# One head of an output projection, loaded by a transfer of 123 rows and one of 5 instead of with its fifteen neighbours

## The chip, the core and the metric

The kernel runs on one core of one Trainium2 chip. The metric is the device time of one execution in microseconds (us). A core has five engines that run side by side, each with its own list of instructions: TensorE (PE, matmuls; its weight loads are shown as PEld), VectorE (DVE), ScalarE (ACT), GpSimd (POOL) and SyncE (SP), which here mostly issues transfers. The transfers themselves run on 16 DMA engines that all queues share. Data is brought from the chip's large memory (HBM) into SBUF, which has 128 partitions; matmul results go to PSUM.

## What is computed

Two independent attention blocks, A and B, with one query token each, decode a cache of 8192 positions; their results stand side by side in the output.

```python
def _A_ref(x, k_cache, v_cache, wq, wo):          # _B_ref: the same with its own arrays
    B, Sq, D = x.shape                             # 1, 1, 512
    H, Dh = 32, 128
    q = (x @ wq).reshape(B, Sq, H, Dh).transpose(0, 2, 1, 3)
    scores = einsum("bhqd,bhkd->bhqk", q, k_cache) * (Dh ** -0.5)   # k_cache: 1, 32, 8192, 128
    p = softmax(scores, axis=-1)
    o = einsum("bhqk,bhkd->bhqd", p, v_cache)
    return o.transpose(0, 2, 1, 3).reshape(B, Sq, H * Dh) @ wo      # wo: 4096 x 512
out = concatenate([a, b], axis=-1)                 # 1, 1, 1024, bf16
```

All inputs are bf16. Each block reads 64 MB of K, 64 MB of V, 4 MB of wq and 4 MB of wo.

## The kernel before

The 32 heads of each block are worked on in tiles of four heads, so there are NM = 16 tiles, n = 0 to 7 for A and 8 to 15 for B. A tile of K or V is 128 partitions by T = 256 positions by 128 numbers: each head fills 32 partitions, and each partition holds 64 KB in one piece of HBM. K has two buffers (`kn`), V one (`vn`).

For each tile, DVE multiplies K by the query in four chunks (`plan_mul`, L343), PE folds the products with an identity matrix (`plan_red`, L352), DVE finishes the sums (`plan_sr`, L363) and takes the maximum, ACT does the exponentials (`plan_exp`, L400). PE then multiplies the probabilities with the V tile in 256 matmuls (`plan_pv`, L421), and DVE scales the result (`plan_o`, L430). PE and DVE run this as loops over the tiles; SP and ACT have it written out.

All loads are issued by SP in a fixed order, in one queue, and each waits on SP until the buffer it overwrites is free. On the DMA engines a queue keeps its order: each engine works through its part of one transfer and then goes on to its part of the next. A transfer over 128 partitions is carried by all 16 DMA engines, eight partitions each.

The end of the order is what the change touches. The two wo arrays are loaded into the K buffer that has come free by then. Block A's wo is one transfer of 32 heads, 32 KB per partition. Block B's wo is cut into groups of heads, `WOG[1]`: heads 0 to 15, then 16 to 23, 24 to 27, 28 and 29, 30, and 31. Within a group of n heads the 128 n rows of wo are dealt to the partitions in runs of n rows, so that each partition holds n KB in one piece; `o` is brought into the same order on PE (`plan_relayout`, L469 to L478) before it is used. SP's order there is: A's wo, B's group 0 (`BEFORE = 1` group), then, when PE is done with the V tile before, the last V tile in two parts (`VLAST`: 192 and 64 positions), then B's groups 1 to 5. Group 0 is used by `plan_wo(1, 0)` (L489), 64 matmuls, ahead of the last V tile; groups 1 to 5 by `plan_wo_rows` (L519), 64 matmuls, behind it. Then DVE copies the result (L530), and it is stored by two transfers of two rows each, one issued by SP and one by ACT (`plan_out`); A's half has been stored earlier in the same way by two transfers from ACT.

`load_wo(a, g)` (L289 to L293) issues the load of one group. It counts up the group's own semaphore, `s_wo[a][g]`, by 16 when the data is there; `wo_in[a, g]` keeps the count to wait for. `dma` (L246, L247) is the helper that issues every transfer, so all of them have L247 in the profile.

Of the kernel before, what the change touches and what calls it, by code (L numbers as in the profile page):

```python
# [11 lines left out]
P = 128  # L12
# [11 lines left out]
class _Plan:  # L24
# [6 lines left out]
    def wait(self, eng, mark):  # L31
        if mark is None:
            return
        ctr, val = mark
        if val <= 0 or self.waited.get((eng, ctr.name), 0) >= val:
            return
        self.waited[(eng, ctr.name)] = val
        self.prog[eng].append((None, ctr, val))

    def op(self, eng, fn, ctr=None, needs=(), inc=1):  # L40

        for m in needs:
            self.wait(eng, m)
        self.prog[eng].append((fn, ctr, inc))
        if ctr is None:
            return None
        ctr.n += inc
        return ctr, ctr.n
# [81 lines left out]
def bass_concat_heads__mha_block_cached__gqa_block_cached__decode_kernel(  # L130
# [21 lines left out]
    NOUT = wos[0].shape[1]  # L152
# [9 lines left out]
    NM = NA * QA  # L162
    NK = 2
    CT = 64
    NCH = T // CT
# [2 lines left out]

    WOG = [[(0, 32)], [(0, 16), (16, 8), (24, 4), (28, 2), (30, 1), (31, 1)]]
    BEFORE = 1  # L170
    HT = [32, 16]
    RG = [32, 16, 8, 4, 2]
    VLAST = (0, T - CT, T)

    with ExitStack() as st:
        ec = st.enter_context

        def sb(name, shape, dt):
            return ec(nc.sbuf_tensor(name, shape, dt))
# [4 lines left out]
        def flat(ap):  # L184
            return ap.rearrange("p t d -> p (t d)")
# [6 lines left out]
        wo_sb = [flat(kn[:, KW])[:, a * W:(a + 1) * W].rearrange("p (j n) -> p j n", n=NOUT)  # L192
                 for a in range(NA)]
# [17 lines left out]
        o2 = sb("o2", [P, NA, H], BF16)  # L211
        oz = sb("oz", [P, H - HT[1], P // 4], BF16)
        mask = {g: sb("mask%d" % g, [P, P // g], BF16) for g in RG}
# [20 lines left out]
        def ctr(name):  # L234
            return _Ctr(nc, st, name)
# [3 lines left out]
        s_wo = [[ctr("s_wo%d%d" % (a, i)) for i in range(len(WOG[a]))] for a in range(NA)]  # L239
# [6 lines left out]
        def dma(eng, dst, src, c, needs=()):  # L246
            return op(eng, lambda e: e.dma_start(dst, src), c, needs, inc=16)  # L247
# [21 lines left out]
        k_in, v_in, wq_in, wo_in = {}, {}, {}, {}  # L269
        red_done, pv_done, q_done, wo_done = {}, {}, {}, {}  # L270
# [18 lines left out]
        def load_wo(a, g):  # L289
            h0, n = WOG[a][g]  # L290
            src = wos[a][h0 * Dh:(h0 + n) * Dh, :].rearrange("(p j) n -> p (j n)", p=P)
            wo_in[a, g] = dma("SP", wo_sb[a][:, h0:h0 + n, :].rearrange("p j n -> p (j n)"), src,
                              s_wo[a][g], [red_done[NM - 2, NCH - 1]])  # L293


        load_wq(0)
# [2 lines left out]
        for a in range(NA):  # L299
# [6 lines left out]
            m = op("PE", xmm, c_pe, [x_in, i_onesb])  # L306
# [122 lines left out]
        def plan_o(n):  # L429
            o_done[n] = op("DVE", lambda e: e.tensor_tensor(  # L430
                oD[:].rearrange("p a h -> p (a h)")[:, nth(n, G)], acc[:, 0:G],
                rinv[:, nth(n), :].rearrange("p o g -> p (o g)"), ALU.mult),
                c_dve, [pv_done[n], r_done[n]])
# [12 lines left out]
        def o_for(a, h0, n):  # L446
            if h0 < HT[a]:
                return o2[:, a, h0:h0 + n]
            return oz[:, h0 - HT[a]:h0 - HT[a] + n, QR - 1]

        def plan_o_rows(a, h0):

            o2_ready[a] = op("DVE", lambda e: e.tensor_copy(o_for(a, h0, H - h0), oD[:, a, h0:H]),
                             c_dve, [i_oz, o_done[NM - 1]])
# [5 lines left out]
        def plan_relayout(*groups):  # L460
            assert len(groups) <= 2
            made = []
            for a, g in groups:
                h0, n = WOG[a][g]
                z = z_n[0] % 2
                z_n[0] += 1
                s = P // n
                zv = zb[:, z, :].rearrange("p (h s) -> p h s", s=s)
                made.append((a, g, h0, n, z, op("DVE", lambda e, a=a, h0=h0, n=n, s=s, zv=zv: e.tensor_tensor(  # L469
                    zv, oD[:, a, h0:h0 + n].unsqueeze(2).broadcast_to([P, n, s]),  # L470
                    mask[n][:, None, :].broadcast_to([P, n, s]), ALU.mult),
                    c_dve, [sel_ready[n], o_done[a * QA + (h0 + n - 1) // G], z_free.get(z)])))
            for a, g, h0, n, z, m in made:
                z_free[z] = op("PE", lambda e, n=n, z=z: e.matmul(  # L474
                    z_ps[z][:, 0:n], zb[:, z, :], jsel[n][:], start=True, stop=True),
                    c_pe, [m, z_read[z][0]])
            for a, g, h0, n, z, m in made:
                o2_ready[a, g] = z_read[z][0] = op("DVE", lambda e, a=a, h0=h0, n=n, z=z: e.tensor_copy(  # L478
                    o_for(a, h0, n), z_ps[z][:, 0:n]), c_dve, [z_free[z], i_oz])

        def plan_wo(a, g):
# [3 lines left out]
            def mm(e):  # L485
                r = None
                for j in range(h0, h0 + n):
                    for i in range(NQ):
                        r = e.matmul(qyp[:, i:i + 1], wo_sb[a][:, j, i * P:(i + 1) * P],  # L489
                                     o2[:, a, j:j + 1], start=(j == 0 and i == 0),  # L490
                                     stop=(j == HT[a] - 1 and i == NQ - 1), skip_group_check=True)
                return r
# [4 lines left out]
        def yrow_of(a):  # L497
            return yrow[:, a * P:(a + 1) * P]

        def plan_turn(a):  # L500

            qy_free[0] = op("DVE", lambda e: e.tensor_copy(
                yT[:].rearrange("p (u r) -> p u r", u=NQ // 2)[:, :, QR - 1:QR + 1],
                qyp[:, 0:NQ].rearrange("p (u r) -> p u r", u=NQ // 2)), c_dve,
                            [i_yT, wo_done[a], yr_done.get(a - 1)])
            yr_done[a] = op("PE", lambda e: e.matmul(
                yrow_of(a), yT[:], ident_f[:], start=True, stop=(HT[a] == H),
                skip_group_check=True), c_pe, [qy_free[0], i_identf])

        def plan_wo_rows(a, g):  # L510

            h0, n = WOG[a][g]

            def mm(e):
                r = None
                for j in range(h0, h0 + n):
                    for i in range(NQ):
                        m = QR - QR * (i % 2) + i % 2
                        r = e.matmul(yrow[i * QR:i * QR + m, a * P:(a + 1) * P],  # L519
                                     oz[:, j - HT[a], QR - m:QR],  # L520
                                     wo_sb[a][:, j, i * P:(i + 1) * P], start=False,
                                     stop=(j == H - 1), skip_group_check=True)
                return r
            yr_done[a] = op("PE", mm, c_pe, [o2_ready[a, g] if n > 1 else o2_ready[a],
                                            wo_in[a, g]])
# [23 lines left out]
        for n in range(NM):  # L549
# [3 lines left out]
            if n + 1 < NM:  # L553
                load_k(n + 1)
            else:
                load_wo(0, 0)
                for g in range(BEFORE):
                    load_wo(1, g)
# [28 lines left out]
        early = [g for g, (h0, n) in enumerate(WOG[1]) if h0 + n <= H - G]  # L587
        for g in range(BEFORE, NB):
            load_wo(1, g)
# [8 lines left out]
        plan_turn(1)  # L598
        plan_relayout(*[(1, g) for g in early[BEFORE:]])
        wait("PE", misc_free[0])  # L600
# [6 lines left out]
        plan_o(NM - 1)  # L607
        plan_wo_rows(1, BEFORE)
        plan_relayout(*[(1, g) for g in range(len(early), NB) if WOG[1][g][1] > 1])
        plan_o_rows(1, WOG[1][NB - 2][0])  # L610
        for g in range(BEFORE + 1, NB):
            plan_wo_rows(1, g)
# [85 lines left out]
```

## Time and profile before

| | |
|---|---|
| median of 3 runs | 666.4 us (666.21 to 666.71) |
| the profiled execution | 666.43 us, its span 665.2 us |
| moved by DMA | 285.33 MB in 6076 packets, mean 429 GB/s |
| busy: PE, PEld, DVE, ACT, POOL | 442.8, 254.9, 340.4, 62.4, 3.0 us |
| mean granted TensorE clock | 0.762 of full speed |

The span reaches from the first instruction of the core to its last; the rest of the execution's time lies around it. Line numbers such as L421 are those of the kernel's file. A row of the timeline gives the start, the duration, the engine, the line, the instruction and the tiles (written<-read), the count, and in brackets the idle time of the engine before it with what ended it. The view of the DMA engines gives, for a window of time that is asked for, the packets that started in it: their number and bytes, how many were under 512 B, 2 KB and 8 KB, and for each queue the time that its packets took as a share of all 16 engines' time. q1 is SP's queue and q10 ACT's; q8 and q14 carry instructions. A row of the table of windows gives the window, its length, then the busy time and number of instructions of PE, PEld, DVE, ACT and POOL, the granted clock, and last the share of time in which the DMA engines were busy (1.00 is all sixteen) and GB/s.

### The profile page before, as it was taken

What the parts mean: (1) busy time and instruction counts of PE and PEld (TensorE: products, weight loads), DVE (VectorE), ACT (ScalarE), POOL (GpSimd) and SP (SyncE); (2) the same over time, 40 slices, a digit from 0 to 9 for tenths busy, and PEclk for the clock granted to TensorE, in tenths of its full rate; (3) what the DMA queues carried; (4) which work ended last, traced back from release to release, by engine and by line L of the source; (5) the groups of instructions that cost most, each with busy time, mean ns of one, the idle gap of its engine ahead of it and who ended that gap; (6) DMA issues with size and microseconds to landing.
All of it is one profiled execution on the core that took longest, in us unless ns stands there. A gap on an engine that the chain in (4) does not pass through costs nothing. (4 is left out here: it accounts for less than half of the span.)

```text
span 665.2 us, 12459 instructions
## 1 busy us (share of the span) xinstructions
PE 442.8 (67%) x5649; PEld 254.9 (38%) x5649; DVE 340.4 (51%) x217; ACT 62.4 (9%) x151; POOL 3.0 (0%) x14
## 2 busy tenths in 40 slices
PE   1165876948487594848759484865948386594885
PEld 0022342615235261614426161442626144262655
DVE  1095809366391836639183663908366380825610
ACT  1002002020201002020100202010020202002020
POOL 1000000000000000000000000000000000000000
PEclk9998857769787766978776597877659787765875
DMA  9999999999999999999999999999999999999997
GB/s 378 441 441 438 438 432 422 418 441 434 434 437 441 441 426 414 441 434 434 437 441 437 426 418 441 434 434 437 441 437 426 418 441 434 434 437 441 404 437 315
DMA packets 6076, 285.33 MB, mean 429 GB/s; under 512 B 690, under 2 KB 948, under 8 KB 1204
## 3 DMA queue, kind: packets, MB, share of 16 engines
q1 hardware_dynamic: 6056, 285.22, 99.3%
q8 instruction: 6, 0.10, 0.1%
q14 instruction: 2, 0.02, 0.0%
q10 hardware_dynamic: 12, 0.00, 0.0%
HBM read 285.21 MB, written 0.00 MB: 429 GB/s over the span
## 5 line engine op out<-in xcount | busy, mean ns | idle before, releaser
L352 PE MATMUL rps<-kn,ident 128*128 128x512 bf16 x1024 | 292.9, 454 | 165.9 <-DVE kn L343 165.9
L343 DVE TENSOR_TENSOR kn<-kn,qbc 128x8192 bf16<-128x8192 bf16 x64 | 281.5, 4419 | 96.1 <-DMA kn<-in_A_k_cache_dram 55.9
L352 PEld LDWEIGHTS rps<-kn,ident 128*128 128x128 bf16 x1024 | 112.2, 113 | 333.6 <-issue 258.3
L421 PE MATMUL acc<-pt,vn 128*128 128x4 bf16 x4096 | 109.4, 165 | 9.8 <-issue 4.1
L421 PEld LDWEIGHTS acc<-pt,vn 128*128 128x128 bf16 x4096 | 108.6, 101 | 10.7 <-DMA vn<-in_B_v_cache_dram 4.5
L363 DVE TENSOR_REDUCE s_sb<-rps 128x64 f32<-128x512 f32 x64 | 44.0, 688 | 110.2 <-PE rps L352 110.2
L400 ACT ACTIVATE pt<-s_sb,negb 32x256 bf16<-32x256 f32 x64 | 54.9, 857 | 1.9
L392 ACT ACTIVATE negb<-bmp 128x1 f32<-128x1 f32 x16 | 2.7, 171 | 529.1 <-PE bmp L388 529.1
L430 DVE TENSOR_TENSOR oD<-acc,rinv 128x4 f32 (+1 forms) x16 | 2.6, 162 | 96.2 <-PE acc L421 85.5
L388 PE MATMUL bmp<-gm,hrow 1*128 1x1 f32 x128 | 18.5, 261 | 6.0 <-DVE gm L378 6.0
L388 PEld LDWEIGHTS bmp<-gm,hrow 1*128 1x128 f32 x128 | 17.2, 204 | 10.7 <-DVE gm L378 10.0
L375 PE MATMUL mtp<-ident_f,m 128*1 128x128 f32 x32 | 6.1, 271 | 19.8 <-DVE m L369 19.8
L400 ACT ACTIVATION_READ_ACCUMULATOR pt<-s_sb,negb 32x1 f32 x64 | 15.9, 248 | 0.0
L375 PEld LDWEIGHTS mtp<-ident_f,m 128*1 128x1 f32 x32 | 1.4, 81 | 27.7 <-DVE m L369 27.7
L303 PE MATMUL misc<-ones_bf,kn 1*128 1x128 bf16 x4 | 0.6, 305 | 13.2 <-DMA kn<-in_B_x_dram 13.2
L378 DVE TENSOR_REDUCE gm<-mtp 1x4 f32<-1x128 f32 x16 | 4.4, 278 | 7.5 <-PE mtp L375 7.5
L405 PEld LDWEIGHTS misc<-rsum,ones_f 128*128 128x128 f32 x32 | 6.2, 197 | 3.6 <-issue 1.4
L321 PE MATMUL qyp<-vn,xb 128*32 128x512 bf16 x64 | 6.0, 504 | 2.2 <-ACT qbc L329 1.5
L369 DVE TENSOR_REDUCE m<-s_sb 128x1 f32<-128x256 f32 x16 | 6.7, 420 | 0.5
L489 PE MATMUL qyp<-o,kn 128*128 128x1 bf16 x192 | 5.5, 165 | 1.0 <-issue 0.8
L489 PEld LDWEIGHTS qyp<-o,kn 128*128 128x128 bf16 x192 | 5.4, 102 | 1.3 <-issue 0.8
L329 ACT CAST qbc<-qyp 128x512 bf16<-128x512 f32 x4 | 2.3, 585 | 37.6 <-PE qyp L321 37.6
(41 smaller groups left out, 31.2 us busy)
## 6 DMA issues: line engine op xcount, KB each, us to landing
vn<-in_B_v_cache_dram SPq DMA_DIRECT2D x1, 6144.0 KB, 21.9
vn<-in_A_wq_dram SPq DMA_DIRECT2D x1, 4096.0 KB, 12.2
vn<-in_B_wq_dram SPq DMA_DIRECT2D x1, 4096.0 KB, 39.7
kn<-in_A_wo_dram SPq DMA_DIRECT2D x1, 4096.0 KB, 35.4
kn<-in_B_wo_dram SPq DMA_DIRECT2D x1, 2048.0 KB, 39.9
vn<-in_B_v_cache_dram SPq DMA_DIRECT2D x1, 2048.0 KB, 26.4
kn<-in_B_wo_dram SPq DMA_DIRECT2D x1, 1024.0 KB, 28.4
kn<-in_B_wo_dram SPq DMA_DIRECT2D x1, 512.0 KB, 29.2
```

The lines of the kernel that those rows point to most:

```text
L321: r = e.matmul(qyp[hh * HP:(hh + 1) * HP, :].rearrange("p (i d) -> p i d", d=Dh), xb[:, a, c, hh * HP:(hh + 1) * HP], w, start=(c == 0), s ...
L343: mul_done[n, c] = op("DVE", lambda e: e.tensor_tensor(k, k, qbc[:, nth(n), :].broadcast_to([P, CT, Dh]), ALU.mult), c_mul, [k_in[n], qbc_ ...
L352: r = e.matmul(rps[:, c % 2, :].rearrange("p (t d) -> p t d", d=DW), ident[:], kn[:, i0, c * CT:(c + 1) * CT, i * DW:(i + 1) * DW], start= ...
L363: sr_done[n, c] = op("DVE", lambda e: e.tensor_reduce(s_sb[:, c * CT:(c + 1) * CT], rps[:, c % 2, :].rearrange("p (t d) -> p t d", d=DW), ...
L369: m_done[n] = op("DVE", lambda e: e.tensor_reduce(m1[:], s_sb[:], AX.X, ALU.max), c_dve, [sr_done[n, NCH - 1]])
L375: m = op("PE", lambda e: e.matmul(mtp[0:1, 0:P], m1[:], ident_f[:], start=True, stop=True), c_pe, [m_done[n], i_identf, gm_done.get(n - 1)])
L378: gm_done[n] = op("DVE", lambda e: e.tensor_reduce(gm[:], mtp[0:1, 0:P].rearrange("o (h p) -> o h p", h=G), AX.X, ALU.max), c_dve, [m, nb_ ...
L388: r = e.matmul(bmp[:, 0:1], hrow[0:1, (G - 1 - h) * HP:(G - 1 - h) * HP + P], gm[0:1, h:h + 1], start=(h == 0), stop=(h == G - 1))
L400: p_done[n] = op("ACT", lambda e, h=h, q=q: e.activation(pt[q, :, h], s_sb[q, :], AF.Exp, bias=negb[q, n:n + 1], scale=scale, accum_out=rs ...
L405: m = op("PE", lambda e: e.matmul(misc[:, 0:G], ones_f[:], rsum[:], start=True, stop=True), c_pe, [p_done[n], misc_free[0]])
L421: r = e.matmul(acc[:, 0:G], vn[:, t, :], pt[:, t, :], start=(t == 0), stop=(t == T - 1))
L489: r = e.matmul(qyp[:, i:i + 1], wo_sb[a][:, j, i * P:(i + 1) * P], o2[:, a, j:j + 1], start=(j == 0 and i == 0), stop=(j == HT[a] - 1 and ...
```

## The change

Head 15 of B's group 0, the last KB of each partition's 16 KB, is taken out of the group's transfer. The first transfer has 15 heads for all 128 partitions. Two more follow it on SP at once: head 15 for partitions 0 to 122, and head 15 for partitions 123 to 127. Both have rows of 1 KB, which lie 16 KB apart in HBM. All three count up the same semaphore, so `wo_in[1, 0]` is now 48 instead of 16. No other group and no other load changes; nothing changes on the other engines but the count that PE waits for ahead of `plan_wo(1, 0)`.

```diff
     BEFORE = 1
+    UNEVEN, FEW = {(1, 0): 1}, [(0, 123), (123, P)]
...
         def load_wo(a, g):
             h0, n = WOG[a][g]
             src = wos[a][h0 * Dh:(h0 + n) * Dh, :].rearrange("(p j) n -> p (j n)", p=P)
-            wo_in[a, g] = dma("SP", wo_sb[a][:, h0:h0 + n, :].rearrange("p j n -> p (j n)"), src,
-                              s_wo[a][g], [red_done[NM - 2, NCH - 1]])
+            dst = wo_sb[a][:, h0:h0 + n, :].rearrange("p j n -> p (j n)")
+            m = n - UNEVEN.get((a, g), 0)
+            parts = [(0, P, 0, m)] + [(p0, p1, m, n) for p0, p1 in FEW if m < n]
+            for p0, p1, j0, j1 in parts:
+                wo_in[a, g] = dma("SP", dst[p0:p1, j0 * NOUT:j1 * NOUT], src[p0:p1, j0 * NOUT:j1 * NOUT],
+                                  s_wo[a][g], [red_done[NM - 2, NCH - 1]])
```

The transfer of 123 rows is carried by three of the DMA engines.

## The prediction

> **What bounds the kernel now.** I read the page from the top: span, the DMA lines of the slices, then the queues.
>
> ```profile
> span 665.2 us, 12459 instructions
> DMA  9999999999999999999999999999999999999997
> GB/s 378 441 441 438 438 432 422 418 441 434 434 437 441 441 426 414 441 434 434 437 441 437 426 418 441 434 434 437 441 437 426 418 441 434 434 437 441 404 437 315
> q1 hardware_dynamic: 6056, 285.22, 99.3%
> ```
>
> The sixteen DMA engines are busy from end to end and the SP queue alone (q1) fills 99.3% of their time; no slice goes over 441 GB/s. The kernel is a stream of 285 MB, and the end is the end of that stream plus a tail. So the next view is the timeline of the last microseconds.
>
> ```profile
> 653.28 7.01 PE L421 MATMUL acc<-pt,vn 128*128 128x4 bf16 x256 [2.96 <-DMA vn<-in_B_v_cache_dram]
> 661.21 1.04 PE L519 MATMUL yrow<-kn,oz 128*32 128x128 bf16 x32 [0.92 <-PEq L619]
> 662.30 1.19 PE L519 MATMUL yrow<-kn,oz 128*32 128x128 bf16 x32
> 663.55 0.29 DVE L530 CAST out_q<-yrow 128x128 bf16<-128x128 f32 x1 [0.90 <-PE yrow L519]
> 663.87 0.27 SPq L247 DMA_DIRECT2D out_dram<-out_q  x1
> ```
>
> PE idles 2.96 us until the first part of the last V tile has landed at 653.3, multiplies for 7.01 us, leaves its loop (0.92 us), takes the 64 wo matmuls, and the output goes out. From 653.3 on little waits for anything else, so the last landing of that V part, on the slowest of the engines that carry it, sets the end; the remaining wo groups follow it in the same queue. A shift of that landing is a shift of the end.
>
> The question is therefore how the sixteen engines stand to each other at that point. A transfer ends on each engine with a 4-byte packet, so I counted the packets under 512 B in windows of the DMA view around the end of the V part (each engine's next packet is 16 KB, its share of the last V rows). Those of q10, the stores of A's output, have to be taken off. The four windows are 650.88 to 651.30, 651.30 to 652.00, 652.00 to 652.60 and 652.60 to 652.82.
>
> ```profile
> DMA packets 20, 0.20 MB, mean 469 GB/s; under 512 B 10, under 2 KB 10, under 8 KB 10
> q10 hardware_dynamic: 2, 0.00, 0.4%
> ...
> DMA packets 13, 0.15 MB, mean 211 GB/s; under 512 B 4, under 2 KB 4, under 8 KB 4
> q10 hardware_dynamic: 3, 0.00, 0.3%
> ...
> DMA packets 20, 0.23 MB, mean 382 GB/s; under 512 B 6, under 2 KB 6, under 8 KB 6
> q10 hardware_dynamic: 1, 0.00, 0.1%
> ...
> DMA packets 8, 0.10 MB, mean 447 GB/s; under 512 B 2, under 2 KB 2, under 8 KB 2
> ```
>
> 10-2, 4-3, 6-1 and 2: eight engines end the V part 1.4 to 1.9 us before the last one, one engine about 1.2 us before it, and seven in the last 0.7 us. The engines have drifted apart, and the late seven set the end. The same spread is there when the queue runs dry: windows of the whole core over the tail (last two numbers: DMA share and GB/s).
>
> ```profile
> 300.00:400.00 100.00, 73.64 (x973) 42.86 (x974) 56.77 (x32) 7.21 (x18) 0.00 (x0) 0.76 1.01 437
> 661.00:661.50 0.50, 0.29 (x15) 0.32 (x19) 0.20 (x2) 0.00 (x0) 0.00 (x0) 0.50 0.61 221
> 661.50:662.00 0.50, 0.50 (x29) 0.48 (x20) 0.26 (x1) 0.00 (x0) 0.00 (x0) 0.50 0.45 166
> 662.00:662.40 0.40, 0.40 (x21) 0.21 (x13) 0.00 (x0) 0.00 (x0) 0.00 (x0) 0.50 0.44 151
> ```
>
> 0.45 x 16 is about seven engines still at work from 661.5 to 662.4, nine idle.
>
> **Which engines are the three.** The profile does not number engines, but a transfer on few engines exists in it: the store of A's output, two rows, in two halves on q10. Its packets appear at two places 0.4 us apart, each beside one engine's 4-byte end of the V part. Windows 651.12 to 651.16 and 651.53 to 651.56:
>
> ```profile
> q10 hardware_dynamic: 2, 0.00, 4.2%
> q1 hardware_dynamic: 1, 0.00, 1.4%
> ...
> q1 hardware_dynamic: 2, 0.02, 129.2%
> q10 hardware_dynamic: 2, 0.00, 5.6%
> ```
>
> So a two-row transfer runs on two engines, one that ends the V part at 651.14 and one at 651.54: 1.6 and 1.2 us before the last, which I put near 652.7. If transfers on few engines always begin with the same ones, these two (I call them a and b) are among the three of the new transfer. The third, c, is one of fourteen: seven early, seven late. The Trainium skill, DMA: Bandwidth & Descriptors, "Why a DMA increments its semaphore by 16 and not by 1", says that a transfer of 127 partitions runs on one engine, that the number is the largest up to 16 that divides the rows, and that the lowest-numbered engines are taken. No run here shows three engines at work; the two of the stores agree with it.
>
> **The change part by part.** The first window of the last table gives one engine's steady rate: 437 / 16 = 27.3 GB/s, 37.5 ns per KB.
>
> Removed: 1 KB of each of an engine's eight rows, 8 x 37.5 = 0.30 us, on all sixteen engines.
>
> Added: 123 rows of 1 KB on three engines, 41 each, and one of the last 5 rows on (I take it) the same three and two more: 42 packets of 1 KB. Their price is in the drain, where the wo groups of one head go as 1 KB packets; window 662.1 to 662.5 of the DMA view:
>
> ```profile
> DMA packets 59, 0.05 MB, mean 133 GB/s; under 512 B 7, under 2 KB 59, under 8 KB 59
> q1 hardware_dynamic: 59, 0.05, 38.4%
> ```
>
> 38.4% of 16 engines in 0.4 us is 2.46 us of packets; 52 of them of 1 KB and 7 of 4 B make at most 47 ns each. Shares above 1 (1.01 in the window above) say that records overlap a little, and 37.5 is the floor, so I take 43 ns: 42 x 43 = 1.81 us. Each heavy engine gains 1.81 - 0.30 = 1.51 us of work (bounds 1.28 to 1.67), ahead of the last V tile and of all that follows it in the queue; the other thirteen lose 0.26 to 0.30 us.
>
> Two more issues on SP, next to the one that is there, and a wait of PE for 48 instead of 16:
>
> ```profile
> 598.82 0.43 SPq L247 DMA_DIRECT2D kn<-in_B_wo_dram  x1
> 631.37 0.80 SPq L247 DMA_DIRECT2D vn<-in_B_v_cache_dram  x2
> ...
> kn<-in_B_wo_dram SPq DMA_DIRECT2D x1, 2048.0 KB, 39.9
> 644.49 1.06 PE L489 MATMUL qyp<-o,kn 128*128 128x1 bf16 x33
> ```
>
> Two issues of 0.43 us end near 600.1; behind them SP's next step, the load of the last V tile, waits for PE until 631.37, so 31 us hide them. The group lands at 598.8 + 39.9 = 638.7; its first use is at 644.49, so even 3 us more stay hidden (were that cover gone, PE's 64 matmuls of about 2 us would be late, and they sit before the V wait with some 3 us to spare). Both at nothing.
>
> The unknown is whether a 1 KB row costs 43 ns when it does not go where that engine's rows usually go. In every transfer of before, an engine writes eight of 128 partitions. Here three engines write 41 each, among them the partitions that the other thirteen are filling at full rate. The drain says that the limit of 27 GB/s is not one of the whole: with 6.1 engines busy (38.4% of 16) they move 133 GB/s, 21.8 each, and none speeds up when others stop. So the limit sits either in the engine, and then the row costs 43 ns, or at the place written, and then two streams halve each other there: a row costs 43 x 2 = 86 ns, less about 0.1 us for rows that fall on b's own partitions. Then a heavy engine gains 3.61 - 0.1 - 0.30 = 3.2 us, and each of the thirteen gives its 0.30 us back while it shares. The trace cannot separate the two, since no two engines meet at one place in it. I hold the dearer a little likelier, because all sixteen run at one equal rate whatever the row size. The Trainium skill, SBUF — State Buffer, "Door 1: The DMA port swizzle", has partitions grouped eight to a port with 16 ports in all, and makes bandwidth a matter of the ports reached; by that rule the row pays the double price. No run so far shows it.
>
> The sum for the likeliest case, sharing with c early: b sets the end, 3.2 - 1.2 = +2.0 us (a 3.2 - 1.6, c 3.2 - 1.7, both less). The profiled execution took 666.43 us around a span of 665.2, and the median of the runs is 666.4: 668.4 us.
>
> **The rivals.**
> - *No sharing, c early:* b again, 1.51 - 1.2 = +0.3, 666.7 us: not slower by what can be told. For it: the 1 KB rows of the drain cost 47 ns at most. Against it: the price of a row among other engines' streams is nowhere in the trace.
> - *No sharing, c late:* the seven late ones stand 0 to 0.6 us before the last, 0.3 in the middle: 1.51 - 0.3 = +1.2, 667.6 us (0.9 to 1.5).
> - *Sharing, c late:* 3.2 - 0.3 = +2.9, 669.3 us.
> - *The gain:* the late engines all lie among the other thirteen and the row costs the floor of 37.5 ns, 42 x 37.5 - 300 = 1.28 us: b comes to +0.1. If b, too, has a lead of 1.6, as a has, b and a end at -0.3, and the late ones' -0.30 is the whole gain, 666.1 us. It decides where all three leads exceed 1.6 us. Nothing here gives more than 0.30 us.
> - *Other engines than I think:* if the transfer goes on three other engines, at least one late one is among them in most draws (nine of sixteen are early), which is the second or third case again.
>
> **How the numbers follow.** A measurement of this kernel can tell about 0.2%, 1.33 us, from no change. Sharing with c early 0.34; sharing with c late 0.28; no sharing with c early 0.18; no sharing with c late 0.16, of which some four parts in ten lie over 1.33 us; the gain 0.04, within 0.2% except for a remainder. Slower: 0.34 + 0.28 + 0.06 = 0.68. Same: 0.18 + 0.10 + 0.02 = 0.30. Faster: 0.02. The range runs from just under the cheap case, 666.5, to just over the dear one, 669.5; it leaves out the gain and rows that cost more than double. The forecast's own range is 667.8 to 669.0.
>
> **What would show it.** Right: DMA windows near 634 to 640 with some 130 packets of 1 KB more, on three engines; the last engine of the V part ending 2 us later, PE's wait before L421 grown from 2.96 to about 5 us, and from L421 on the same durations as before. In the tail, one to three engines at work after the other thirteen are dry. A 1 KB packet near 46 ns with +0.3 or +1.2 us on that wait shows that the places written don't share. Wrong altogether: the V part landing on time, or a change in PE's wait that is not the change in the span; the new rows on one engine or on all sixteen; or the wait for 48 holding PE at 644.

## The result and the profile after

The changed kernel takes 667.8 us (667.67 to 668.04, 19 runs) against 666.52 us (19 runs) before: ratio 1.0019, 95% interval [1.0013, 1.0026], 1.3 us slower. The profiled execution took 667.79 us around a span of 666.5 us; before it was 666.43 around 665.2.

The page says that the same bytes went through the same queue; only the packets are more, 6212 for 6076.

```profile
span 666.5 us, 12461 instructions
DMA packets 6212, 285.33 MB, mean 428 GB/s; under 512 B 698, under 2 KB 1084, under 8 KB 1340
q1 hardware_dynamic: 6192, 285.22, 99.2%
```

The timeline of the last microseconds, with the rows that answer to those of before:

```profile
648.40 0.99 PE L494 MATMUL qyp<-o,kn 128*128 128x1 bf16 x31 [2.23 <-issue]
...
654.63 7.01 PE L426 MATMUL acc<-pt,vn 128*128 128x4 bf16 x256 [2.22 <-DMA vn<-in_B_v_cache_dram]
662.61 1.04 PE L524 MATMUL yrow<-kn,oz 128*32 128x128 bf16 x32 [0.96 <-PEq L624]
663.70 1.15 PE L524 MATMUL yrow<-kn,oz 128*32 128x128 bf16 x32
664.90 0.29 DVE L535 CAST out_q<-yrow 128x128 bf16<-128x128 f32 x1 [0.86 <-PE yrow L524]
```

The matmuls with the last V tile begin at 654.63 instead of 653.28, 1.35 us later, and from there every step takes what it took before (7.01, 1.04, 1.15 for 1.19). All of the loss lies ahead of the landing of the V part.

How the engines end that part, from the DMA view: windows 651.30 to 652.00, 652.00 to 653.10, 653.10 to 653.40 and 654.00 to 654.20 (none end between the last two).

```profile
DMA packets 19, 0.25 MB, mean 351 GB/s; under 512 B 8, under 2 KB 8, under 8 KB 8
q10 hardware_dynamic: 1, 0.00, 0.1%
...
DMA packets 25, 0.33 MB, mean 298 GB/s; under 512 B 7, under 2 KB 7, under 8 KB 7
q10 hardware_dynamic: 1, 0.00, 0.1%
...
DMA packets 14, 0.16 MB, mean 547 GB/s; under 512 B 4, under 2 KB 4, under 8 KB 4
q10 hardware_dynamic: 2, 0.00, 0.6%
...
DMA packets 7, 0.07 MB, mean 329 GB/s; under 512 B 3, under 2 KB 3, under 8 KB 3
q10 hardware_dynamic: 2, 0.00, 0.8%
```

8-1, 7-1, 4-2 and 3-2: seven, six, two, and one last engine alone near 654.1. Two packets of q10 stand beside that last one, and two beside the pair at 653.2, so these are the two engines that carry the store of A's output: a near 653.2, and b last. In the trace of before b ended at 651.54 with 1.2 us to spare. The trace keeps start, length, size and queue of every packet, and a packet that begins as another ends is taken to be on the same engine. By these packet records the last of the middle six ends at 653.01, where the last engine of before ended at 652.74: engines that carry 8 KB less and no row of the new transfers are later too.

Why even they are later shows in the middle of the move. Windows of the whole core from 636.40 to 639.40, while the 1 KB rows run; before and, below it, after:

```profile
636.40:639.40 3.00, 1.39 (x10) 0.75 (x9) 1.79 (x5) 0.00 (x0) 0.00 (x0) 1.00 1.10 475
```

```profile
636.40:639.40 3.00, 1.39 (x9) 0.58 (x7) 1.79 (x5) 0.00 (x0) 0.00 (x0) 1.00 0.98 334
```

In the same window the DMA engines are almost as busy and move 334 GB/s instead of 475. Packets are booked where they start, so a window of 3 us says this only roughly: `no_rows` below, which loads no row of head 15, has 390 in the same window. The length of a single packet is firmer. The share in a DMA view, times 16 engines, times the window, is the time of the packets that start in it. Here are two windows of 2 ns in which one 48 KB packet of the V tile starts, 636.372 to 636.374 before and 636.394 to 636.396 after:

```profile
q1 hardware_dynamic: 1, 0.05, 5671.9%
...
q1 hardware_dynamic: 1, 0.05, 7450.0%
```

That is 1.82 us before and 2.38 after. By the packet records the first such packet of each of the thirteen engines without the new rows takes 2.22 to 2.40 us, where all sixteen took 1.82 before and take 1.82 to 1.83 in no_rows. So every one of the thirteen is slowed, by 22 to 32%.

The DMA view of after from 637.0 to 638.2 gives the price of a row:

```profile
DMA packets 73, 0.35 MB, mean 294 GB/s; under 512 B 6, under 2 KB 65, under 8 KB 65
```

65 - 6 = 59 rows of 1 KB in 1.2 us on three engines: 61 ns each, between the 43 and the 86 that the prediction had as its two prices.

### The profile page after: what moved, and what is told of

It reads as the page before. It is cut to its first block, busy times and chain, and to the rows that moved or that the text cites. A ratio compares the mean times of both kernels' runs of the same rounds, so it can differ in the third digit from the quotient of the medians.

```text
span 666.5 us, 12461 instructions
## 1 busy us (share of the span) xinstructions
PE 446.7 (67%) x5649; PEld 255.4 (38%) x5649; DVE 340.5 (51%) x217; ACT 62.4 (9%) x151; POOL 3.0 (0%) x14
## 2 busy tenths in 40 slices
DMA packets 6212, 285.33 MB, mean 428 GB/s; under 512 B 698, under 2 KB 1084, under 8 KB 1340
## 5 line engine op out<-in xcount | busy, mean ns | idle before, releaser
L357 PE MATMUL rps<-kn,ident 128*128 128x512 bf16 x1024 | 297.9, 460 | 164.1 <-DVE kn L348 164.1
```

Source lines behind the costliest of these rows:

```text
L357: r = e.matmul(rps[:, c % 2, :].rearrange("p (t d) -> p t d", d=DW), ident[:], kn[:, i0, c * CT:(c + 1) * CT, i * DW:(i + 1) * DW], start= ...
```

## The experiments

Three theories were tried first. P (place): rows are slow and slow others because three engines write where the other engines write. H (pitch): the rows lie 16 KB apart in HBM, and reading them holds all up. E (engines): what matters is only that a few engines have many 1 KB rows more, wherever these go. For the end, B says that b sets it; its rivals are A (any heavy engine would) and C (the third engine, c, does).

**split_even: head 15 by itself, on all sixteen engines**

```diff
-    UNEVEN, FEW = {(1, 0): 1}, [(0, 123), (123, P)]
+    UNEVEN, FEW = {(1, 0): 1}, [(0, P)]
```

> Head 15 goes by itself, but as one transfer of 128 rows on all 16 engines, 8 rows each; nothing uneven is left. The profile of the changed kernel shows every engine, heavy or not, slowed by about a quarter from 636.4 to 639.4 us (334 GB/s instead of 437) while the 1 KB rows run. Theory P (place): the rows are slow and slow the others because three engines write where the other thirteen write. Here each engine writes its own partitions, so: 0 to +0.1 us over before, 437 GB/s throughout, ratio 1.000. Theory H (pitch): the rows are slow because 1 KB pieces 16 KB apart in HBM are read, and that holds all readers up. Here 128 such rows are read as well: the same dip of GB/s for 2 to 3 us and +0.4 to +0.8 us on every engine and on the end, ratio 1.0006 to 1.0012. Theory E (engines): only the 42 rows on one engine matter; no dip, +0.0.

Measured: 666.52 us, ratio 1.0001 [0.9992, 1.0010]. Its window from 636.40 to 639.40:

```profile
636.40:639.40 3.00, 1.39 (x9) 0.60 (x8) 1.79 (x5) 0.00 (x0) 0.00 (x0) 1.00 1.22 514
```

No dip and no loss, with 128 rows of 1 KB read 16 KB apart; the first V packet of each engine takes 1.82 to 1.86 us. Taking the head out of its transfer, and 1 KB rows as such, cost nothing that can be told. H is badly hurt; P and E stand.

**rows_adjoin and rows_pitch15: other distances in HBM**

```diff
+                rows = src[p0:p1, j0 * NOUT:j1 * NOUT]
+                if j0:
+                    rows = wos[a][p0 * 1:p1 * 1, :].rearrange("(p j) n -> p (j n)", j=1)[:, 0:NOUT]
```

(15 in place of the three 1s for rows_pitch15; `rows` is then the source.)

> As the changed kernel, but the 123 and 5 rows are read from the first 128 rows of B's wo, which lie side by side in HBM, instead of 16 KB apart (head 15's weights are thus other rows of wo). Engines and places written are the same. Theory P (place): nothing changes, 667.8 us, dip to 334 GB/s. Theory H (pitch): no dip, a row costs 43 ns instead of 57 to 59, the thirteen others end 0.3 us earlier than before instead of 0.5 later, and the slowest heavy engine adds 1.5 us minus its lead of 0.8 to 1.2: 666.8 to 667.2 us.

> As the changed kernel, but the rows are read 15 KB apart in HBM instead of 16 KB (head 15's weights are other rows of wo). Theory P: 667.8 us and the dip. Theory H, if what hurts is a distance of a power of two: as rows side by side, 666.8 to 667.2 and no dip. Theory H, if what hurts is any 1 KB row that stands alone: 667.8 and the dip.

Measured: 667.94 us, ratio 1.0021 [1.0012, 1.0030], and 667.81 us, ratio 1.0020 [1.0011, 1.0029]. The window of rows_adjoin (rows_pitch15 has 340 GB/s in the same):

```profile
636.40:639.40 3.00, 1.39 (x8) 0.48 (x7) 1.67 (x5) 0.00 (x0) 0.00 (x0) 1.00 1.01 347
```

The same time and the same dip with rows side by side, and the thirteen first V packets take 2.18 to 2.35 us here too. H has fallen: where the rows are read from makes no difference.

**no_rows: the most that relief can bring**

```diff
-    UNEVEN, FEW = {(1, 0): 1}, [(0, 123), (123, P)]
+    UNEVEN, FEW = {(1, 0): 1}, []
```

> Head 15 is not loaded at all (what lies in the buffer is used for it); the transfer of 15 heads is as in the changed kernel. This is the most that relieving the thirteen engines can bring: 8 KB at 37.5 ns each, -0.30 us against before under every theory, 666.2 us, ratio 0.9995. If the end does not move, the chain behind the V tile is not set by the late engines as the prediction took it.

Measured: 666.16 us, ratio 0.9995 [0.9986, 1.0004]. The median moved by -0.34 us, near the expected -0.30, but the interval holds no change. This is what any redistribution of these 8 KB could gain at best.

**only_a and a_and_b: which heavy engine sets the end**

```diff
-    UNEVEN, FEW = {(1, 0): 1}, [(0, 123), (123, P)]
+    UNEVEN, FEW = {(1, 0): 1}, [(0, 41)]
```

(82 in place of the 41 for a_and_b.)

> As the changed kernel, but of head 15 only the first 41 rows are loaded, by one transfer, which one engine carries (the other 87 rows of head 15 are left out). The engine is taken to be a, which ended the V part 1.6 us before the last in the trace of before. Theory B (the end of the changed kernel is set by b, whose lead was 0.8 to 1.2 us; a and c are covered by theirs): a takes 41 rows of 43 to 58 ns, 1.8 to 2.4 us, less 0.3, less its lead of 1.6: -0.1 to +0.5, against before: 666.4 to 667.0. Rival C (c is one of the late engines and sets the end, or any heavy engine does): c and b are not heavy here, the same figure. Rival A (leads don't matter, a heavy engine ends late wherever it stood): 667.8 as in the changed kernel.

> As before, but 82 rows of head 15, 41 each on two engines, a and b (46 rows are left out). Theory B: b has less lead than a, so the end is that of the changed kernel or a little less, as fewer rows collide: 667.4 to 667.9. Rival C: with c spared, the end falls back to 666.4 to 667.0.

Measured: 666.88 us, ratio 1.0004 [0.9995, 1.0013], and 667.89 us, ratio 1.0019 [1.0010, 1.0028]. With 41 rows on a alone the kernel is within what can be told of before; with 41 more on b the whole loss of the change is there, without any row on c. The starts of the V matmuls agree (only_a, then a_and_b):

```profile
653.79 7.01 PE L426 MATMUL acc<-pt,vn 128*128 128x4 bf16 x256 [1.70 <-DMA vn<-in_B_v_cache_dram]
```

```profile
654.80 7.01 PE L426 MATMUL acc<-pt,vn 128*128 128x4 bf16 x256 [2.21 <-DMA vn<-in_B_v_cache_dram]
```

B holds. A has fallen with only_a, where one heavy engine costs 0.3 us; only_a alone could not tell B from C, and C has fallen with a_and_b. That the heavy engine of only_a is a can be seen in its trace: the packets of A's store stand beside the ends of the V part at 651.62, near b's 651.54 of before, and at 653.27, the last end of all. This also shows, from outside the trace, that a lead covers work: 41 rows are nearly free on a, and 41 more on b cost 1.0 us.

**own_place and other_place: the same rows, two places**

```diff
-    UNEVEN, FEW = {(1, 0): 1}, [(0, 123), (123, P)]
+    UNEVEN, FEW = {(1, 0): 8}, []
...
+            for p0 in [0 + i for i in (0, 1, 2, 3, 32, 33, 34, 35)] if m < n else []:
+                rows = wos[a][0:n * P, :].rearrange("(p j) n -> p j n", j=n)
+                wo_in[a, g] = dma("SP", wo_sb[a][p0:p0 + 9:4, h0 + m:h0 + n, :], rows[p0:p0 + 9:4, 0:n:2, :],
+                                  s_wo[a][g], [red_done[NM - 2, NCH - 1]])
```

(64 in place of the 0 in `0 + i` for other_place.)

> The transfer on all engines has 8 heads only. Then 64 rows of 1 KB on each of three engines, by eight transfers of three partitions with 8 rows each, into partitions 0 to 11 and 32 to 43. By the Trainium skill, DMA: Bandwidth & Descriptors, section The descriptor swizzle, these are the partitions that the first three engines write anyway. (Heads 8 to 15 are left out in the other 104 partitions.) All engines lose 8 KB in each of eight rows, 2.4 us; the three heavy ones gain 64 rows. Theory P (place): rows at 43 ns, 2.75 us, no dip of GB/s while they run; b ends 0.35 us later, less its lead of 0.8 to 1.2: the end moves by -0.45 to -0.85, 665.7 to 666.1. Theory E (any 1 KB rows on few engines slow all of them): rows at 57 to 59 ns, 3.7 us, the dip to some 340 GB/s for 3.7 us; +0.1 to +0.5, 666.6 to 667.0.

> As the kernel with own places, but the same eight transfers go to partitions 64 to 75 and 96 to 107, which by the same section of the Trainium skill three other engines write, and which those fill meanwhile with the V tile. Theory P: rows at 58 to 86 ns, 3.7 to 5.5 us, with a dip of GB/s; the end moves by 3.7 - 2.4 - 0.8 to 1.2 = +0.1 to +0.5 with the lower price and +1.9 to +2.3 with the higher: 666.6 to 668.8, and at least 0.7 us over the kernel with own places. Theory E: the same time as with own places within 0.2 us.

Measured: 665.92 us, ratio 0.9990 [0.9981, 0.9999], and 668.71 us, ratio 1.0033 [1.0020, 1.0045]: 2.8 us apart, for rows of the same number, size and engines. Windows of the whole core from 636 to 640, own_place and then other_place:

```profile
636.00:640.00 4.00, 2.12 (x17) 1.23 (x16) 2.06 (x7) 0.39 (x2) 0.00 (x0) 1.00 1.09 462
```

```profile
636.00:640.00 4.00, 2.39 (x15) 1.13 (x13) 1.79 (x5) 0.00 (x0) 0.00 (x0) 1.00 0.95 227
```

And the DMA view for the price of a row: own_place from 635 to 636.5, other_place from 636 to 638.

```profile
DMA packets 130, 0.72 MB, mean 482 GB/s; under 512 B 16, under 2 KB 114, under 8 KB 114
```

```profile
DMA packets 83, 0.51 MB, mean 254 GB/s; under 512 B 10, under 2 KB 74, under 8 KB 74
```

98 rows in 1.5 us on three engines is 46 ns each; 64 rows in 2 us is 94 ns each. E has fallen: rows on few engines cost 46 ns and trouble nobody as long as they go where those engines write anyway, and double where other engines write. That the place decides is shown. Whether it does so because another engine is filling it at that time, or only because it is not the engine's own, is not separated: no run writes to the place of an engine that is idle. What P had not said is how far the trouble reaches. In other_place the rows go to 24 of 128 partitions; were only the three engines that write there slowed, the ten others alone would move 10 x 27.3 = 273 GB/s. The core as a whole moved 227. The packet records say it outright: of the thirteen engines without rows, each has a 48 KB packet that starts between 635.3 and 637.1 and takes 3.46 to 3.57 us, about twice the 1.82 to 1.83 of own_place. (own_place is no faster version: it leaves out most of heads 8 to 15.)

## Why the prediction was right, and where its size was off

**The bound, the path and the end** were right. The landing of the V part sets the end: it moved by 1.35 us and the end by 1.3, with every step behind it unchanged. Splitting alone cost nothing (split_even). The forecast's sign in the tail came as well: the DMA engines are busy for a share of 0.13 from 663.0 to 663.5 and 0.07 from 663.5 to 664.0, two engines and then one.

**Which engine** was right: b, with its lead of 1.2 us, ends last and alone, and c did not matter. Taking the two engines of the store for two of the three was the step that carried this; only_a and a_and_b confirm it. That c is an early engine (by the packet records it is the one that ends beside a, near 653.2) was luck: the prediction gave its two cases with c early 0.52 and those with c late 0.44. The Trainium skill's rule that lowest-numbered engines are taken (DMA: Bandwidth & Descriptors, "Why a DMA increments its semaphore by 16 and not by 1") agrees with these runs as far as a profile that does not number engines can show it: the engines of the store carry the rows in only_a and a_and_b.

**Sharing** was the right side of the open question, but the price was mis-sized and the mechanism only half right. The prediction took 86 ns a row, because two streams halve each other at the place where they meet, and let the thirteen others lose no more than the 0.30 us they had gained. A row cost 61 ns while all three engines were at work, and all thirteen were slowed together, though three engines write to a few places at a time only (other_place shows the same more strongly).

The packet records close the sum for b. It begins its rows at 636.91, where before it began the V tile at 637.01: -0.10 us in place of the forecast -0.30. Of the missing 0.20, b reached the group 0.09 us later, and 0.11 went to its own 15 KB packets, the last of which were slowed. The 42 rows last until 639.40, 2.49 us or 59 ns each, in place of 3.5. Its V part takes 14.71 us instead of 14.53, +0.18 in place of nothing. Less the lead of 1.20 that makes +1.37, beside the measured 1.35. The term for the others was too small as well: the late engines lost their 0.30 us and about 0.3 more (652.74 to 653.01).

Why a row costs 61 ns here and 94 in other_place was not tried. One difference is that here each row of an engine goes to another partition, while there its 64 rows go to eight partitions, eight rows in sequence to each.

So 668.4 was 0.6 us too high. The measured time falls nearest to the rival without sharing and with c late (667.6), whose mechanism is not what happened: its c did not set the end, and the rows did share. The time alone would have picked the wrong story. It also lies just inside the 0.2% that the chances were cut at, where 0.68 had been given to more and 0.30 to no change that can be told. And the range of 666.5 to 669.5 held every rival but the gain, so that the result lies in it says little.

**PE's wait** ahead of the V matmuls was forecast to grow to about 5 us and shrank to 2.22: PE came to it later, after an idle of 2.23 us (released by "issue") in the middle of its wo matmuls at 648.40, which was 0.75 before. It is covered by the wait for V either way. The prediction had named a change in this wait that is not the change in the span as a sign that it was wrong altogether. The sign came, but it was badly chosen: the wait also depends on when PE arrives, and the landing itself moved with the span. What makes the idle longer was not tried; it is not the wait for the count of 48, since no_rows, which waits for 16, has 2.40 us there.

## What to carry to other kernels

Moving bytes from late DMA engines to early ones means writing to places that other engines fill; here such rows cost 61 to 94 ns instead of 46, and every engine slowed down with them. Before rebalancing, load nothing at all once (no_rows): here the ceiling was 0.34 us and the attempt cost 1.3. A lead is a budget of one engine, not of the early group: b's 1.2 us was spent by 42 rows where a's 1.6 us nearly covered as many.

## What the hardware showed that was not expected

Three engines that write into partitions other engines are filling slow the whole core's transfers, not only the engines concerned: 227 GB/s over four microseconds instead of 462, and 48 KB packets of 3.46 to 3.57 us instead of 1.82 on all thirteen others. One engine is enough to be seen: in only_a the first V packets of the fifteen others take 1.94 to 2.13 us. By what path the slowing spreads was not tried.

Part of the engines' spread comes from packets that carry instructions. Before, q8 has a 16 KB packet at 643.87 (1.06 us) and one at 651.06 (1.10 us), and each holds up one engine; the second alone makes its engine one of the seven late ones.

A transfer on few engines can hold SP for long. The three issues of B's group 0 in the changed kernel (minimum, median and maximum in ns):

```profile
L248 SPq DMA_DIRECT2D kn<-in_B_wo_dram x3: 308/433/8587, 597.5 to 598.4; - x3
```

The last of them held SP for 8.6 us, where the prediction had 0.43. It cost nothing here, since SP's next step waits until 630.72. In own_place, with eight transfers on three engines, one issue held SP for 19.9 us. What it waits for was not tried; the single transfers of only_a and a_and_b, on one and two engines, took 0.29 us to issue.
